# Weights made in thirds between the attention's steps, and four raw weight loads moved behind the chunks' loads

## The chip, the cores and the metric

The kernel runs on one core of a Trainium2 chip. The metric is the device time of one execution in microseconds (us). A core has TensorE (PE, the matrix engine), VectorE (DVE), ScalarE (ACT), GpSimd (POOL) and SyncE (SP, whose queue issues the loads here). Each engine works through its own instructions in the order in which the program gives them, and waits on semaphores for what other engines or DMAs produce.

## The reference

Decayed linear attention over 2 x 768 tokens with 8 heads of 64, then a gated layer (512 to 1536 to 512) behind a root-mean-square norm, then a three-way maximum layer (512 to 768 to 512), all in 32-bit floats:

```python
def _attn_ref(q, k, v, lam) -> np.ndarray:
    ...
    for b in range(nb):
        sl = slice(b * block, (b + 1) * block)
        qb, kb, vb = (q[:, :, sl], k[:, :, sl], v[:, :, sl])
        intra = np.einsum('bhic,bhjc->bhij', qb, kb) * Dmask[None]
        intra = np.einsum('bhij,bhjd->bhid', intra, vb)
        inter = np.einsum('bhid,bhde->bhie', qb * lam_pow[None], kv_state)
        out[:, :, sl] = intra + inter
        rev_pow = lam[:, None, None] ** (block - 1 - pos[None, :, None])
        kb_dec = kb * rev_pow[None]
        kv_state = lam_block[None, :, None, None] * kv_state + np.einsum('bhsd,bhse->bhde', kb_dec, vb)
    return out.astype(np.float32)

def _moe_ref(x, w_gate, w_val, w_out, rms_g) -> np.ndarray:
    rms = np.sqrt(np.mean(x * x, axis=-1, keepdims=True) + 1e-06)
    xn = x / rms * rms_g
    g = xn @ w_gate
    silu = g * (1.0 / (1.0 + np.exp(-g)))
    val = xn @ w_val
    return (silu * val @ w_out).astype(np.float32)

def _moe2_ref(x, w1, w2, w3, w_out) -> np.ndarray:
    h = np.maximum(np.maximum(x @ w1, x @ w2), x @ w3)
    return (h @ w_out).astype(np.float32)
```

## The kernel before

**Attention.** The 1536 tokens are 12 chunks of 128. Each chunk passes nine steps: `T` turns k and q on PE (`turn`, tiles `pk`, `pq`), `C` makes scores, `a` and `b` mask them on DVE into the two halves of `A`, `M` mixes (`px`), `S` carries the state (`pS`, `S_kv`), `U` sums squares (`ms`, and `ri` on POOL), `N` norms (`pb`, `x` on DVE, `xh` on ACT) and `R` makes the rest `xl`. The steps of neighbouring chunks are interleaved in one list, and `attn_step` takes the next. All matrix products of the two layers are made of three: high part by high, high by low, low by high (`mm3`: L425, L426, L427), so every operand has a `...h` and a `...l` tile.

**First stage.** For each block of 512 tokens and each of the first six hidden tiles `f`, `hidden1` makes `pg` and `pv`, Silu (L571) and the product `sg` (L572); `split` makes `hh` on ACT and `hl` on POOL; `out1` adds into `acc`, which is drained to `acc_sb` (L454 to L456). The attention steps that the first block needs run ahead of the first stage, the others in the *gaps*: `gap()` is called twice in every product of a hidden tile and twice in `out1`. The last six hidden tiles and the maximum layer are the *second stage*: products of halves (`p`, `r`, `q`, L637), with sums of weights (`tsum`, L181, L203) and sums of x (`sums`, L494), and ACT copies `c` out of `p` and `r` (L692) that must be done before PE goes on with the same bank.

**Weights.** A weight *unit* is 128 columns or rows of a matrix, named here by matrix and tile: g1, v6, o6 are tile 1 of `w_gate`, tile 6 of `w_val`, tile 6 of `w_out`; T units are sums. It is loaded as raw integer words (`wraw`, 512 KB, three buffers, L149). `begin_unit` asks for raw loads and issues two ACT steps (L227, L228). `words_of_unit` has three parts on DVE: L188, L191 and L194, the last with POOL's add (L196). `finish_unit` copies `wh` on ACT (L157) and makes `wl` on POOL (L160), or on DVE for some sums (L173). `make_unit` does all of that for one unit after another at once (finish of the unit before, the three parts of the current one, begin of the next); `third_of_unit` does it in three calls. Before, `make_unit` is called at four attention steps and in the gaps of the first eight steps of the first stage and the next four, `third_of_unit` in all later gaps.

**Order.** There is no scheduler: the order of the code is the order on every engine. What sets it around the change is the list of attention steps at which raw words are loaded and units made (L921 to L924), the rule in `gap()` (L408 to L413), the three parts in `third_of_unit` (L250 to L252), and on the load queue the order of `loads_to` (k, q and v of a chunk: `kn`, `qn`, with three buffers each, `vn` with four, L90) and `load_to` (L149).

Of the kernel before, what the change touches and what calls it, by code (L numbers as in the profile page):

```python
# [26 lines left out]
def tile_decay_attention_swiglu_maxout(  # L27
# [85 lines left out]
    groups1 = [4, 2]  # L113
# [23 lines left out]
    stage1, stage2 = [], []  # L137
# [15 lines left out]
    def finish_unit(key, W, at):  # L153
        if key:
            wh = wpools[at].tile([P, 512], F32R, tag="wh", name="wh")
            wl = wpools[at].tile([P, 512], F32R, tag="wl", name="wl")
            nc.scalar.copy(out=wh, in_=W.bitcast(F32))  # L157
            if second_sum(key):
                return lambda: lower_of_sum(key, W, wh, wl)
            nc.gpsimd.tensor_tensor(out=wl, in0=W.bitcast(F32), in1=wh.bitcast(F32), op=ALU.subtract)  # L160
            units[key] = (wh, wl)
# [14 lines left out]
    def copy_partner():  # L176
        if stage1 and first_sum(stage1[-1][0]):
            other = partner(stage1[-1][0])
            if other not in sums_in:
                sums_in[other] = psum.tile([P, 512], I32, tag="bank", name="tsum")  # L180
                nc.scalar.copy(out=sums_in[other].bitcast(F32), in_=words[other].bitcast(F32))  # L181
# [46 lines left out]
            nc.scalar.activation(out=lo, in_=lo.bitcast(U32), func=AF.Copy, scale=2.0 ** -29)  # L228
            stage1.append((key, W, at, lo, hi))

    def make_unit():

        if stage2:
            finish_unit(*stage2.pop(0))
        if stage1:
            unit = stage1.pop(0)
            for n in range(3):
                words_of_unit(n, *unit)
            stage2.append(unit[:3])
        begin_unit()  # L240

    thirds = []

    def third_of_unit():

        if not thirds:
            done = stage2.pop(0) if stage2 else (None,) * 3
            unit = stage1.pop(0) if stage1 else (None,) * 5
            later = []
            thirds.extend([lambda: (begin_unit(), words_of_unit(0, *unit)),  # L250
                           lambda: (later.append(finish_unit(*done)), copy_partner(), words_of_unit(1, *unit)),
                           lambda: (later[0] and later[0](), words_of_unit(2, *unit), stage2.append(unit[:3]))])  # L252
        thirds.pop(0)()

# [148 lines left out]
    def gap():  # L403


        pos["gap"] += 1
        if not pos["quiet"]:
            if pos["step"] == len(steps) or pos["step"] >= groups1[0] * NBLK and pos["gap"] % 4:  # L408
                third_of_unit()
            elif pos["step"] >= groups1[0] * NBLK:  # L410
                pass
            elif (pos["gap"] + 5) % (2 if pos["step"] < groups1[0] else 4) == 0:
                make_unit()  # L413
        due.sort(key=lambda e: e[0])
        while due and due[0][0] <= pos["gap"]:
            due.pop(0)[1]()
        if gaps[0]:
            left = sum(1 for p in attn_q if p[0] <= gaps[1])
            for _ in range(-(-left // gaps[0])):
                attn_step()  # L420
            gaps[0] -= 1
# [472 lines left out]
    with tc.manual_schedule():  # L894
        nc.scalar.dma_start(out=lam8, in_=lam.rearrange("(o h) -> o h", o=1).to_broadcast([P, H]))
        loads_to(0)
        nc.scalar.dma_start(out=g_sb, in_=rms_g.rearrange("(a p) -> p a", p=P))
        make_identity(nc, ident)
        nc.vector.memset(ones, 1.0)
        nc.vector.memset(zeros, 0.0)  # L900
        nc.scalar.activation(out=mhalf, in_=zeros[:, 0:1], func=AF.Silu)
        nc.vector.memset(mhalf, -0.5)
        warm = bank("warm")
        for i in range(9):
            nc.tensor.matmul(out=warm[:, 0:P], lhsT=zeros, rhs=zeros, start=True, stop=True)
        nc.gpsimd.memset(S_kv, 0.0)
        for h in range(H):
            nc.vector.tensor_tensor_scan(
                out=Tm[:, h, :], data0=lam8[:, h:h + 1].to_broadcast([P, P]), data1=ident,
                initial=0.0, op0=ALU.mult, op1=ALU.add)  # L910
        for hf in range(2):
            nc.vector.tensor_copy(out=lamh[64 * hf:64 * hf + 64, :],
                                  in_=lam8.rearrange("p (a t) -> p t a", t=2)[64 * hf:64 * hf + 64, hf, :])
        for a in range(NP):
            nc.vector.tensor_tensor_scan(
                out=lami[:, a, :], data0=lamh[:, a:a + 1].to_broadcast([P, P]), data1=zeros,
                initial=1.0, op0=ALU.mult, op1=ALU.add)
        loads_to(1)
        for i in range(sum(1 for p in attn_q if p[0] <= CPNB + 2)):
            attn_step()  # L920
            if i in (0, 7, 8, 17, 25, 40, 41, 48):  # L921
                load_to(pos["load"] + 1)
            if i in (15, 22, 32, 47):
                make_unit()  # L924
        finish = first_stage()
        pos["step"] = len(steps)
        second_stage(finish)
# [31 lines left out]
```

## Time and profile before

| what | value |
|---|---|
| median of 3 runs | 564.85 us (564.38 to 565.11) |
| the profiled execution | 567.43 us, its span 564.5 us |
| PE busy in the span | 547.1 us (97%) |
| DVE, ACT, POOL busy | 383.1 us (68%), 272.0 us (48%), 320.7 us (57%) |
| mean granted clock of PE | 0.989 |

All rows below come from that one profiled execution; times in them count from the start of its span. A row of the timeline gives start, duration, engine, line, operation, output and inputs by the program's names, and in brackets how long the engine stood idle before it and what ended that. A row of the windows gives the busy time of each engine in one stretch, the clock granted to PE (1.00 is 2.4 GHz, 0.50 is 1.2 GHz) and the share of the DMA engines.

### The profile page before, as it was taken

To read this page: it belongs to the slowest core of one execution; us is meant where nothing else is said; L and a number is where in the kernel's file an instruction comes from. 1 tells how busy PE (TensorE), PEld (TensorE's weight loads), DVE (VectorE), ACT (ScalarE), POOL (GpSimd) and SP (SyncE) were. 2 spreads that over 40 slices of the span, in tenths; PEclk is the share of its full clock that TensorE was granted. 3 is DMA by queue.
4 is the path that set the end of the run, shared out by engine and by line. 5 is a ranking of instruction groups with operands and counts; after the bars stand their busy time and mean duration, and the time that the engine had idled before them with its cause. 6 is when DMAs were issued, how large, how long until landed. Compare 5 with 4: busy or idle time off the path is not lost.

```text
span 564.5 us, 7794 instructions
## 1 busy us (share of the span) xinstructions
PE 547.1 (97%) x2880; PEld 452.0 (80%) x2880; DVE 383.1 (68%) x583; ACT 272.0 (48%) x517; POOL 320.7 (57%) x256
## 2 busy tenths in 40 slices
PE   7979989999999999989999999999999999999997
PEld 7968767888788888778888888878888888888885
DVE  6687997423358789686676867896567567774364
ACT  3566754332354534446626455555465755552120
POOL 2577998311167677647727747687377553962050
PEclk9998999999999999989999999999999999999999
DMA  8767646000023211212312222120222322210014
GB/s 204 189 177 188 176 134 168 1 0 1 2 81 107 72 40 35 66 48 76 113 38 74 75 74 76 37 75 1 74 75 76 96 91 75 74 39 0 2 45 178
DMA packets 64646, 44.54 MB, mean 79 GB/s; under 512 B 39264, under 2 KB 60768, under 8 KB 64608
## 3 DMA queue, kind: packets, MB, share of 16 engines
q1 hardware_dynamic: 63936, 44.05, 26.6%
q8 instruction: 22, 0.36, 0.3%
q14 instruction: 16, 0.13, 0.1%
q10 hardware_dynamic: 672, 0.01, 0.1%
HBM read 40.90 MB, written 3.15 MB: 78 GB/s over the span
## 4 chain that ended last, share of the span: by engine, by line
PE 83%; DVE 9%; DMA 2%; ACT 2%; issue 1%; POOL 1%; SPq 0%; ACTq 0%; DVEq 0%
PE p L637 27%; PE r L637 7%; PE acc L425 5%; PE acc L427 5%; PE acc L426 5%; PE q L637 4%; PE acc L820 3%; PE acc L819 3%; PE acc L821 3%; PE pg L425 3%; PE pg L426 3%; PE pg L427 2%; PE pv L425 2%; PE pv L427 2%; PE pv L426 2%; PE px L322 2%
## 5 line engine op out<-in xcount | busy, mean ns | idle before, releaser
L160 POOL TENSOR_TENSOR wl<-W,wh 128x512 fp32r<-128x512 f32 x75 | 102.8, 1371 | 43.4 <-ACT wh L157 43.3
L196 POOL TENSOR_TENSOR W<-W,wraw 128x512 int32<-128x512 int32 x60 | 80.7, 1346 | 72.6 <-DVE W L194 70.8
L157 ACT CAST wh<-W 128x512 fp32r<-128x512 f32 x75 | 46.5, 620 | 68.0 <-POOL W L196 67.8
L439 POOL TENSOR_TENSOR hl<-sg,hh 128x512 fp32r<-128x512 f32 x36 | 48.8, 1356 | 43.5 <-ACT hh L438 43.5
L425 PE MATMUL acc<-hh,wh 128*128 128x512 f32 x144 | 57.2, 397 | 1.0 <-DVE xl L447 1.0
L426 PE MATMUL acc<-hl,wh 128*128 128x512 f32 x144 | 56.2, 390 | 0.0
L427 PE MATMUL acc<-hh,wl 128*128 128x512 f32 x144 | 56.1, 390 | 0.0
L637 PE MATMUL p<-xl,wh 128*128 128x512 f32 x120 | 46.7, 389 | 0.0
L637 PE MATMUL p<-xh,wh 128*128 128x512 f32 x120 | 46.7, 389 | 0.0
L637 PE MATMUL p<-xh,wl 128*128 128x512 f32 x120 | 46.7, 389 | 0.0
L227 ACT ACTIVATE W<-wraw 128x512 f32<-128x512 f32 x60 | 40.0, 667 | 9.6 <-POOL wl L160 5.6
L438 ACT CAST hh<-sg 128x512 fp32r<-128x512 f32 x36 | 22.3, 620 | 43.6 <-DVE sg L572 37.4
L228 ACT ACTIVATE wraw<-wraw 128x512 int32<-128x512 uint32 x60 | 39.7, 661 | 0.0
L439 POOL TENSOR_TENSOR hl<-m,hh 128x512 fp32r<-128x512 f32 x18 | 24.5, 1366 | 24.2 <-ACT hh L438 24.1
L637 PE MATMUL p<-yh,wh 128*128 128x512 f32 x90 | 35.0, 389 | 0.0
L637 PE MATMUL p<-yl,wh 128*128 128x512 f32 x90 | 35.0, 389 | 0.0
L637 PE MATMUL p<-yh,wl 128*128 128x512 f32 x90 | 35.0, 389 | 0.0
L692 ACT COPY c<-p 128x512 f32<-128x512 f32 x30 | 17.7, 588 | 33.5 <-PE p L637 33.4
L425 PEld LDWEIGHTS acc<-hh,wh 128*128 128x128 f32 x144 | 27.0, 188 | 7.5 <-DVE xl L447 1.8
L792 DVE TENSOR_TENSOR acc_sb<-acc,acc_sb 128x512 f32<-128x512 f32 x34 | 23.3, 690 | 14.1 <-PE acc L427 13.3
L188 DVE TENSOR_SCALAR mid<-W 128x512 f32<-128x512 f32 x37 | 25.4, 686 | 9.3 <-ACT W L227 4.7
L427 PEld LDWEIGHTS acc<-hh,wl 128*128 128x128 f32 x144 | 27.0, 188 | 5.8
(177 smaller groups left out, 1444.2 us busy)
## 6 DMA issues: line engine op xcount, KB each, us to landing
wraw<-in_moe_w_out_dram SPq DMA_DIRECT2D x18, 512.0 KB, 3.4
wraw<-in_moe_w_dram SPq DMA_DIRECT2D x18, 512.0 KB, 3.6
wraw<-in_moe_w_gate_dram SPq DMA_DIRECT2D x12, 512.0 KB, 3.6
wraw<-in_moe_w_val_dram SPq DMA_DIRECT2D x12, 512.0 KB, 3.6
kn<-in_k_dram SPq DMA_DIRECT2D x12, 256.0 KB, 4.1
qn<-in_q_dram SPq DMA_DIRECT2D x12, 256.0 KB, 4.4
vn<-in_v_dram SPq DMA_DIRECT2D x12, 256.0 KB, 4.7
out_dram<-acc_sb SPq DMA_DIRECT2D x12, 256.0 KB, 2.0
```

The source lines that it names most:

```text
L157: nc.scalar.copy(out=wh, in_=W.bitcast(F32))
L160: nc.gpsimd.tensor_tensor(out=wl, in0=W.bitcast(F32), in1=wh.bitcast(F32), op=ALU.subtract)
L188: nc.vector.tensor_scalar(out=mid[key].bitcast(F32), in0=W.bitcast(F32), scalar1=LEAST, scalar2=MOST, op0=ALU.max, op1=ALU.min)
L196: nc.gpsimd.tensor_tensor(out=W, in0=W, in1=lo, op=ALU.add)
L227: nc.scalar.activation(out=W.bitcast(F32), in_=hi.bitcast(F32), func=AF.Abs)
L228: nc.scalar.activation(out=lo, in_=lo.bitcast(U32), func=AF.Copy, scale=2.0 ** -29)
L425: nc.tensor.matmul(out=out, lhsT=wh, rhs=xh_, start=first, stop=False)
L426: nc.tensor.matmul(out=out, lhsT=wh, rhs=xl_, start=False, stop=False)
L427: nc.tensor.matmul(out=out, lhsT=wl, rhs=xh_, start=False, stop=last)
L439: nc.gpsimd.tensor_tensor(out=dst_l, in0=src, in1=dst_h.bitcast(F32), op=ALU.subtract)
L637: nc.tensor.matmul(out=ps, lhsT=w[:, ks], rhs=r[:, o + k, :], start=first and k == 0 and n == 0, stop=k == 1 and n == 2, skip_group_check= ...
L792: nc.vector.tensor_tensor(out=ps if kept else y, in0=ps, in1=y, op=ALU.add)
```

## The change

`make_unit` is gone, and every unit is made by thirds. Between attention steps there are thirteen thirds where four whole units were; in the gaps of the first steps two gaps take three thirds together, and later four gaps take three, which is the old rate. Within a unit's thirds `finish_unit` moves from the second third to the first and `begin_unit` from the first to the second, everywhere in the kernel. Raw loads are asked for at other attention steps.

```diff
--- before.py
+++ after.py
@@ -228,17 +228,6 @@
             nc.scalar.activation(out=lo, in_=lo.bitcast(U32), func=AF.Copy, scale=2.0 ** -29)
             stage1.append((key, W, at, lo, hi))
 
-    def make_unit():
-
-        if stage2:
-            finish_unit(*stage2.pop(0))
-        if stage1:
-            unit = stage1.pop(0)
-            for n in range(3):
-                words_of_unit(n, *unit)
-            stage2.append(unit[:3])
-        begin_unit()
-
     thirds = []
 
     def third_of_unit():
@@ -247,8 +236,8 @@
             done = stage2.pop(0) if stage2 else (None,) * 3
             unit = stage1.pop(0) if stage1 else (None,) * 5
             later = []
-            thirds.extend([lambda: (begin_unit(), words_of_unit(0, *unit)),
-                           lambda: (later.append(finish_unit(*done)), copy_partner(), words_of_unit(1, *unit)),
+            thirds.extend([lambda: (later.append(finish_unit(*done)), words_of_unit(0, *unit)),
+                           lambda: (begin_unit(), copy_partner(), words_of_unit(1, *unit)),
                            lambda: (later[0] and later[0](), words_of_unit(2, *unit), stage2.append(unit[:3]))])
         thirds.pop(0)()
 
@@ -409,8 +398,9 @@
                 third_of_unit()
             elif pos["step"] >= groups1[0] * NBLK:
                 pass
-            elif (pos["gap"] + 5) % (2 if pos["step"] < groups1[0] else 4) == 0:
-                make_unit()
+            else:
+                for _ in range((1, 2)[pos["gap"] % 2] if pos["step"] < groups1[0] else (0, 1, 1, 1)[pos["gap"] % 4]):
+                    third_of_unit()
         due.sort(key=lambda e: e[0])
         while due and due[0][0] <= pos["gap"]:
             due.pop(0)[1]()
@@ -918,10 +908,9 @@
         loads_to(1)
         for i in range(sum(1 for p in attn_q if p[0] <= CPNB + 2)):
             attn_step()
-            if i in (0, 7, 8, 17, 25, 40, 41, 48):
-                load_to(pos["load"] + 1)
-            if i in (15, 22, 32, 47):
-                make_unit()
+            for _ in range((15, 15, 15, 18, 20, 22, 27, 30, 34, 40, 42, 45, 47).count(i)):
+                third_of_unit()
+            load_to(pos["load"] + (0, 7, 8, 30, 39, 47, 47).count(i))
         finish = first_stage()
         pos["step"] = len(steps)
         second_stage(finish)
```

The load queue (SP), from the `vn` of chunk 4 on. `kn`, `qn`, `vn` belong to one chunk each, in order (chunks 5 and 6 and the first of 7 here); the `wraw` rows are g1 and v1. Before:

```order
L90 DMA vn_252<-in_v_dram 128x8x64
L149 DMA wraw_326<-in_moe_w_gate_dram 128x4x256
L90 DMA kn_338<-in_k_dram 128x8x64
L90 DMA qn_340<-in_q_dram 128x8x64
L90 DMA vn_342<-in_v_dram 128x8x64
L149 DMA wraw_417<-in_moe_w_val_dram 128x4x256
L90 DMA kn_430<-in_k_dram 128x8x64
L90 DMA qn_432<-in_q_dram 128x8x64
L90 DMA vn_434<-in_v_dram 128x8x64
L90 DMA kn_524<-in_k_dram 128x8x64
```

Now:

```order
L90 DMA vn_252<-in_v_dram 128x8x64
L90 DMA kn_337<-in_k_dram 128x8x64
L90 DMA qn_339<-in_q_dram 128x8x64
L90 DMA vn_341<-in_v_dram 128x8x64
L90 DMA kn_431<-in_k_dram 128x8x64
L90 DMA qn_433<-in_q_dram 128x8x64
L90 DMA vn_435<-in_v_dram 128x8x64
L149 DMA wraw_480<-in_moe_w_gate_dram 128x4x256
L90 DMA kn_522<-in_k_dram 128x8x64
```

The raw words of g1 stood ahead of chunk 5 and those of v1 ahead of chunk 6; now both chunks stand ahead of g1, and v1 comes behind chunk 7.

ACT, at the passage from the first stage to the second. `W_2152` is v6 and `W_2202` is o6; `xh<-sums` are sums of x, `sg<-pg` is the last Silu of the first stage, `c` are the copies out of `p` and `r`, `W_2103` is a sum of weights. Before:

```order
L498 CAST xh_687<-sums_2163 128x512
L498 CAST xh_687<-sums_2206 128x512
L571 ACTIVATE sg_2257<-pg_2219 128x512
L438 CAST hh_2260<-sg_2257 128x512
L157 CAST wh_2274<-W_2152 128x512
L181 COPY tsum_2278<-W_2152 128x512
L692 COPY c_2297<-p_2290 128x512
L692 COPY c_2308<-r_2301 128x512
L157 CAST wh_2310<-W_2202 128x512
L692 COPY c_2329<-p_2290 128x512
L227 ACTIVATE W_2333<-wraw_2150 128x512
```

Now (v6 is `W_2156`, o6 is `W_2207`, the sum `W_2107`; lines stand 10 or 11 lower):

```order
L488 CAST xh_692<-sums_2167 128x512
L157 CAST wh_2241<-W_2156 128x512
L181 COPY tsum_2253<-W_2156 128x512
L488 CAST xh_692<-sums_2211 128x512
L561 ACTIVATE sg_2264<-pg_2224 128x512
L428 CAST hh_2267<-sg_2264 128x512
L157 CAST wh_2289<-W_2207 128x512
L682 COPY c_2303<-p_2296 128x512
L682 COPY c_2313<-r_2306 128x512
L157 CAST wh_2323<-W_2107 128x512
L682 COPY c_2333<-p_2296 128x512
L227 ACTIVATE W_2337<-wraw_2154 128x512
```

The copy `wh` of v6 and its `tsum` now stand ahead of Silu, `wh` of o6 ahead of the first copy `c`, and `wh` of the sum between the copies.

## Rows read from the trace of the kernel before

**Rows 1.** The page's head and its first part: busy us, share, instructions.

```profile
span 564.5 us, 7794 instructions
...
PE 547.1 (97%) x2880; PEld 452.0 (80%) x2880; DVE 383.1 (68%) x583; ACT 272.0 (48%) x517; POOL 320.7 (57%) x256
```

**Rows 2.** PE's waits over the span: for what, us in total, times, longest.

```profile
PE pv L425 <- DVE x L378: 2.0, 1, 2.0
PE q L637 <- DVE acc_sb L456: 2.0, 1, 2.0
...
PE pb L376 <- POOL ri L367: 1.3, 1, 1.3
...
PE pk L273 <- DMA kn<-in_k_dram: 1.2, 1, 1.2
```

**Rows 3.** Busy times by stretch: stretch, us, busy us by engine, clock, DMA share.

```profile
41.00:48.00 7.00, 6.27 (x28) 5.38 (x29) 5.68 (x7) 3.08 (x6) 5.52 (x5) 0.54 0.80 181
...
60.00:95.00 35.00, 31.03 (x234) 24.70 (x230) 32.27 (x41) 18.79 (x41) 31.59 (x26) 1.00 0.61 160
95.00:190.00 95.00, 94.67 (x529) 77.54 (x530) 44.43 (x62) 39.04 (x77) 36.34 (x29) 1.00 0.12 39
190.00:231.00 41.00, 41.00 (x183) 33.93 (x181) 38.06 (x44) 17.38 (x33) 27.73 (x19) 1.00 0.12 39
...
241.00:246.00 5.00, 4.28 (x12) 3.39 (x13) 3.76 (x7) 2.23 (x5) 1.22 (x1) 0.66 0.00 0
```

The busy columns are PE, PE's weight loads, DVE, ACT and POOL.

**Rows 4.** Timeline of the load queue, 28 to 38 us.

```profile
28.72 0.37 SPq L149 DMA_DIRECT2D wraw<-in_moe_w_gate_dram  x1
...
37.37 0.46 SPq L90 DMA_DIRECT2D kn<-in_k_dram  x1
```

**Rows 5.** Timeline of PE at chunk 6's turn.

```profile
41.73 1.11 PE L273 MATMUL pk<-ident,kn 128*128 128x128 f32 x4 [1.16 <-DMA kn<-in_k_dram]
```

**Rows 6.** Timeline of POOL at `xl` of chunk 3.

```profile
40.84 1.27 POOL L389 TENSOR_TENSOR xl<-x,xh 128x512 fp32r<-128x512 f32 x1 [2.21 <-ACT xh L380]
```

**Rows 7.** Timeline of DVE, 33 to 71 us.

```profile
33.33 0.43 DVE L191 TENSOR_SCALAR W<-W 128x512 int32<-128x512 int32 x1
...
45.58 1.03 DVE L188 TENSOR_SCALAR W<-W 128x512 f32<-128x512 f32 x1 [1.21 <-ACT W L227]
...
68.04 1.40 DVE L191 TENSOR_SCALAR W<-W 128x512 int32<-128x512 int32 x1
...
70.09 0.69 DVE L305 TENSOR_TENSOR A<-sc,Tm 128x512 f32<-128x512 f32 x1
```

**Rows 8.** Timeline of ACT at the passage, 230 to 239 us.

```profile
230.41 0.59 ACT L571 ACTIVATE sg<-pg 128x512 f32<-128x512 f32 x1
...
233.34 0.58 ACT L692 COPY c<-p 128x512 f32<-128x512 f32 x1
...
237.65 0.62 ACT L157 CAST wh<-W 128x512 fp32r<-128x512 f32 x1 [3.25 <-POOL W L196]
```

**Rows 9.** Timeline of PE at the passage, 233 to 242 us.

```profile
233.97 0.50 PE L637 MATMUL p<-zh,wh 128*128 128x512 f32 x1
...
241.72 0.60 PE L637 MATMUL q<-xh,wh 128*128 128x512 f32 x1 [1.98 <-DVE acc_sb L456]
```

**Rows 10.** Timeline of DVE ahead of and in the passage, 204 to 241 us.

```profile
204.33 0.69 DVE L572 TENSOR_TENSOR sg<-pv,sg 128x512 f32<-128x512 f32 x1 [1.22 <-POOL zl L447]
...
227.65 1.27 DVE L456 TENSOR_TENSOR acc_sb<-acc,acc_sb 128x512 f32<-128x512 f32 x2
...
229.78 0.68 DVE L194 SCALAR_TENSOR_TENSOR W<-wraw,W 128x512 int32<-128x512 int32 x1
...
240.38 0.70 DVE L188 TENSOR_SCALAR mid<-W 128x512 f32<-128x512 f32 x1 [4.63 <-ACT sg L713]
```

**Rows 11.** The page's groups of POOL's add and `hl`: count, busy, mean ns, idle.

```profile
L196 POOL TENSOR_TENSOR W<-W,wraw 128x512 int32<-128x512 int32 x60 | 80.7, 1346 | 72.6 <-DVE W L194 70.8
L439 POOL TENSOR_TENSOR hl<-sg,hh 128x512 fp32r<-128x512 f32 x36 | 48.8, 1356 | 43.5 <-ACT hh L438 43.5
```

## The prediction

> **What bounds the kernel now.** I read the page's busy times first [rows 1]: TensorE (PE) is busy 547.1 us of the span of 564.5, so what a change of order alone can give is the 17.4 us in which PE waits, and what the clock loses beside them. Then PE's own waits [rows 2]: 1.3 us for POOL's `ri`, 1.2 us for a load of `kn`, and 2.0 us each for DVE's `x` and `acc_sb`. Third, the busy times by stretch [rows 3]: between 41 and 48 us the granted clock averages 0.54, near the lower of its two levels (1.2 of 2.4 GHz), right after the two waits for `ri` and `kn`; between 241 and 246 us it averages 0.66, after the wait for `acc_sb`. The same rows show DVE busy 32.27 of 35 us and POOL 31.59 of 35 between 60 and 95 us, with PE at 31.03: there the bound is DVE's queue. From 95 to 190 us PE is busy 94.67 of 95 us, and from 190 to 231 it never waits. So three places decide: the turn of chunk 6 at 41 us, DVE's queue to 95 us, and the passage from the first stage to the second at 231 to 246 us. PE's own instructions keep their order, and every engine executes the same set of instructions as before; only waits move.
>
> **Part 1, the loads.** The load queue is served in order. The raw words of g1 are issued at 28.72 us, when a raw buffer comes free, and chunk 5's `kn` stands right behind them; chunk 6's `kn` is issued at 37.37 behind the words of v1 [rows 4]. Its data are what PE waits 1.2 us for at 41.73 [rows 5]. After the change both chunks stand ahead of g1. Their own buffers are free by about 23 to 28 us (three buffers of `kn`, four of `vn`), so both loads go out some seven and ten us early, and this wait goes: -1.2 us. The raw words move behind three and six loads of 256 KB; g1's own buffer is free only at 28.7 us, so they lose little, and v1 is needed by PE more than ten us later. I cost the later raw words at nothing; the cover is that slot wait, and without it a raw load would come one chunk's landing later for ScalarE (ACT), 4.4 us by the time from 37.37 to the end of the wait at 41.73 [rows 4, 5], not for PE.
>
> **Part 2, thirds in the attention.** POOL's `ri` of chunk 3 stood behind the integer add and a whole unit's `wl` on POOL; PE waits 1.3 us for it [rows 2]. In thirds `wl` of g0 starts as soon as its `wh` does, some three us earlier, and the queue ahead of `ri` is shorter; chunk 5's earlier `qn` also moves the steps ahead of it by about 1 us. I take the whole 1.3 us away, and at worst 0.5. With both waits gone I take it that the clock does not fall: 6.27 busy us at a mean of 0.54 instead of 1.00 cost 6.27 x 0.46 = 2.9 us [rows 3]. Gross: 1.2 + 1.3 + 2.9 = 5.4 us. What is late next: `pg` needs `xl` of chunk 3, which POOL makes from 40.84 on [rows 6], ending at 42.11. That hangs on `pb` through `x` and `xh` and so moves by `pb`'s 1.3 to 2.2 us only, while PE would now arrive at about 40.1: a new wait between 0 and 1.7 us, taken as 1.0. PE is then some 4.4 us early at 60 us.
>
> **Part 3, DVE's queue from 45 to 95 us.** This takes part of it back. DVE runs nearly without a break there, and PE waits for it: the second half of `A` at 70.09 [rows 7], `x` for 2.0 us [rows 2]. DVE gains only what it stood still for: 1.21 us before 45.58 [rows 7], which hangs on `W`'s first ACT step behind the copy of the late `pk`, 2.7 us of standing in 60 to 95 (35 less 32.27), and what it begins earlier at 44 us. The most is therefore about 5.4 us, the least about 0.5, if the raw integer steps that now stand between the attention's steps (`L188`, `L191`, `L194` one by one) come just ahead of an `A` or `x` that PE wants. I take 3.0, nearer to the row of the 1.21 us plus the earlier start than to either end. From 95 us on PE has no wait up to 231, so 3.0 us are carried that far.
>
> A step of DVE's costs two prices: `L191` 0.43 us at 33.33 and 1.40 us at 68.04 [rows 7], the long one while POOL works. The Trainium skill ("SBUF — State Buffer", section "SBUF: two separate sides") calls the ports of these two engines an exclusive lock, held for a whole instruction, with the loser blocked. The row agrees, and this speaks against the change: three more such meetings in the stretch would cost 3 x 0.97 = 2.9 us, all that the start keeps, and the sum would be +1.6 instead of -1.3.
>
> **Part 4, inside a third.** The two ACT steps that begin a unit move from the first third to the second, and the copy `wh` from the second to the first. So `wh` stands one gap behind POOL's add instead of two: ACT now waits for POOL more often, with what is queued behind. In most places PE has well over 1 us of reserve, and I cost them at nothing (0 to 1 us for all). At 231 us there is none. Before, ACT's Silu ran at 230.41 and the copy `c` at 233.34 to 233.92, both ahead of the next `wh` at 237.65, which waited 3.25 us for POOL [rows 8]; PE started `p` 0.05 us after that copy, at 233.97 [rows 9]. After, `wh` of v6 with its `tsum` stands ahead of Silu and `wh` of o6 ahead of the copy. Call t the end of DVE's `L194` of v6, 230.46 before [rows 10]. From t it goes through POOL's add (1.35 [rows 11]), `wh`, `tsum`, `xh` and Silu (0.58 to 0.62 each by the kinds in [rows 8], less about 0.1 of overlap between neighbours) to about t + 3.6, and on through `sg` (0.69 [rows 10]), `hh` (0.62), `hl` (1.36), the add of o6 (1.35 [rows 11]), `wh` (0.62) and the copy (0.58) to about t + 8.6. `L191` now goes before four `acc_sb` steps, the last two of which ended at 227.65 + 1.27 = 228.92 [rows 10], and `L194` right behind them: with both set in, at 0.41 and 0.68 us, t is about 230.0. DVE stood twice for 1.2 us earlier in that stretch (one of the two before 204.33 [rows 10]); without either, t is 227.6. Taking t = 229.0, the copy ends at 237.6 instead of 233.9: PE loses 3.7 us there (0.05 of reserve aside). Against that, the 2.0 us at 241.72 [rows 9] go: PE arrives later than the `acc_sb` that it waited for. That `acc_sb` stood behind `mid` at 240.38, after a stop of 4.63 us [rows 10]. Net 3.7 - 2.0 = +1.7 us, with t from 227.6 to 230.0 from +0.3 to +2.7. The clock's fall after 241 us (4.28 busy us at 0.66 instead of 1.00, 1.5 us) I expect again, only earlier; it could vanish (-1.5) or be worse (+1.5).
>
> **Sum.** -3.0 + 1.7 + 0 = -1.3 us. The profiled execution took 567.43 us, 2.9 of it around the span, and lies 2.6 over the median of the runs shown (564.85); nothing in the sum hangs on that, so I put it against the median: 564.85 - 1.3, rounded to 563.5.
>
> **Rivals.** (a) *The gain stays whole.* DVE follows PE and Silu is in time: -5.0 at the start, +0.3 in the middle, 560.1 us. For it: DVE stood 2.7 us in 60 to 95. Against: PE already waited for DVE there three times. (b) *Slower: ACT is held by `wh` at 231 to 239 us.* t = 230.0 gives 2.7 us, the clock falls for longer (1.5), and DVE keeps only 1.0 of the start: +3.2, 568.0 us. It decides the sign from the point where t + 8.6 is more than the start's kept gain plus 2.0 behind 233.9, so with 1.0 kept from t = 228.3 on, with 3.0 kept from t = 230.3 on. For it: `c` had 0.05 us of reserve. (c) *DVE takes it back:* the start keeps 1.5, and the middle costs 1.7: 565.0, no change. (d) *The clock falls at 41 us as before,* since PE idles for `xl` up to 1.7 us: the start keeps 1.0 and the time is 565.5. For it: two stops of 1.3 and 1.2 were enough before; against: the 2.0 us for `x` [rows 2] left the clock of 60 to 95 at 1.00 [rows 3]. The Trainium skill ("TensorE: Matmul & The Clock Gate", section "What's actually happening") calls the low level the default, released by activity; the fall after the waits agrees, and by it (d) would need PE to be no busier there than before. (e) *It does nothing:* the added moves are hidden and c6's load was the only effect: within 0.2%, as (c).
>
> **How the numbers follow.** A measurement of this kernel can tell about 0.2%, 1.1 us, from no change; so faster is under 563.7 and slower over 566.0. Forecast 0.35 (0.25 of it faster, 0.10 the same), (a) 0.20 faster, (c) with (e) 0.22 (0.03, 0.16, 0.03), (d) 0.08 (0, 0.04, 0.04), (b) 0.15 slower. That makes faster 0.48, same 0.30, slower 0.22. The range reaches from (a) with 0.3 us more to most of (b): 559.8 to 567.3; the likeliest case's own is 562 to 565.
>
> **What would show it.** In the changed profile: no wait for `kn` on `pk` and none or little for `ri` on `pb`, the clock near 1.00 in 36 to 46 us (part 1, 2); a wait for `xl` on `pg` near 40 us under 1.7; the second half of `A` of chunk 7 at 66 to 69 instead of 70.09 (part 3); Silu at 231 to 234 and `c` ending at 236 to 239 minus the start's gain, a wait of PE for ACT's `c` or Silu near 231 to 235, and none for `acc_sb` at 241 (part 4). The forecast is wrong if PE is more than 4 us or less than 1 us early at 200 us, or if PE does not wait for ACT at the passage.

## The result and the profile after

The changed kernel takes 571.65 us (median of 6 runs, 569.01 to 572.25); the kernel before, on the same chip, 564.98 (6 runs, 564.38 to 567.22). The ratio is 1.0105 with a 95% interval of 1.0078 to 1.0131: about 6 us slower, where the forecast was 1.3 us faster, and above the top of its range (567.3). The profiled execution of the changed kernel took 572.25 us, with a span of 569.2.

In the profiles below, lines above 230 stand 10 or 11 lower than before: L415 to L417 are L425 to L427, L627 is L637, L561 is Silu (L571), L682 the copy `c` (L692), L367 is `x` (L378), L369 `xh` (L380), L378 `xl` (L389). First PE's waits in the changed kernel, as in [rows 2]:

```profile
PE p L627 <- ACT c L682: 2.7, 2, 2.2
PE pq L264 <- ACT sg L561: 2.0, 1, 2.0
PE acc L415 <- DVE xl L437: 1.5, 2, 1.0
PE px L311 <- DVE A L294: 1.4, 3, 0.6
PE pg L415 <- ACT xh L369: 1.3, 1, 1.3
PE r L627 <- ACT sg L561: 1.2, 1, 1.2
...
PE pg L416 <- POOL xl L378: 0.9, 1, 0.9
PE acc L416 <- POOL hl L429: 0.8, 1, 0.8
```

The four waits of [rows 2] are gone: `ri` and `kn` at chunk 6's turn, `x` at 79 us, `acc_sb` at 241. In their place PE waits for ACT, 5.9 us for `c` and Silu, and for `xh`, `xl` and `hl`. The busy times by stretch, as in [rows 3], and for 41 to 48 and 241 to 246 us also those of a second profile of the kernel before (the run b2_before, below), which come last, in a fence of their own:

```profile
41.00:48.00 7.00, 5.46 (x31) 4.43 (x32) 6.93 (x8) 4.47 (x9) 6.11 (x5) 0.76 0.68 174
...
60.00:95.00 35.00, 31.99 (x214) 24.76 (x212) 28.18 (x40) 18.94 (x40) 30.46 (x26) 0.95 0.58 155
...
231.00:241.00 10.00, 6.61 (x23) 4.70 (x22) 3.61 (x8) 4.69 (x10) 8.31 (x7) 0.87 0.34 107
```

```profile
41.00:48.00 7.00, 6.27 (x39) 5.19 (x40) 5.82 (x7) 3.46 (x7) 5.31 (x5) 0.76 0.75 170
...
241.00:246.00 5.00, 5.00 (x22) 4.15 (x23) 4.93 (x9) 2.37 (x5) 0.48 (x2) 1.00 0.00 0
```

In the second profile the clock averages 0.76 at 41 us where the first had 0.54, and 1.00 at 241 us where the first had 0.66. The same waits are there in both: 1.2 or 1.3 us each for `ri` and `kn`, 2.0 for `acc_sb`.

PE's instructions stand in the same order in both kernels and in all that follow (but for one or two pairs of neighbours, at 23 and 36 us), so one number tells where time is lost: the start of an instruction in one profile less its start in the second profile of before. In us, at some instructions (named by their start in that profile):

| kernel | 35 | 50 | 82 | 90 | 100 | 228 | 236 | 250 | 365 | 495 |
|---|---|---|---|---|---|---|---|---|---|---|
| before, first profile | +0.2 | +0.9 | +0.8 | +0.8 | +0.8 | +0.8 | +0.8 | +2.4 | +2.4 | +2.4 |
| changed | -0.8 | +0.0 | -0.8 | +3.1 | +1.2 | +1.2 | +6.6 | +4.7 | +5.8 | +7.1 |
| e1: load order alone | -0.5 | -2.4 | -0.4 | -0.4 | -0.4 | -0.4 | -0.4 | +1.2 | +1.2 | +1.3 |
| e3: inside of a third alone | +1.9 | +0.2 | +3.1 | +3.1 | +1.2 | +1.4 | +4.3 | +3.4 | +3.4 | +7.7 |
| e4: old inside from step 13 on | -0.8 | -0.1 | -0.9 | +1.5 | +0.4 | +0.4 | +3.9 | +2.0 | +2.0 | +3.6 |
| e5: as e4, twelve thirds | -0.7 | +0.1 | +1.2 | +1.9 | +2.4 | +2.4 | +2.6 | +2.7 | +2.7 | +2.7 |
| e13: one `wh` behind Silu | -0.8 | +0.0 | -0.9 | -0.3 | +1.4 | +1.4 | +5.3 | +3.5 | +4.6 | +6.9 |
| e14: one `wh` behind `c` | -0.6 | +0.2 | -0.7 | +3.3 | +1.4 | +1.4 | +2.7 | +2.2 | +3.3 | +5.5 |
| e16: `L188` behind `x` | -0.7 | -2.6 | -1.9 | +2.1 | +0.1 | +0.2 | +5.6 | +3.7 | +4.8 | +7.0 |
| e7: drain ahead of the third | +0.2 | -0.2 | +1.9 | +1.9 | +0.0 | +0.0 | -0.2 | -2.5 | -2.5 | -2.5 |

Up to 100 us the first profile of before, e3 and e7 execute what the second does, and yet stand 0.8, 1.2 and 0.0 us later there: that much differs between executions, and a fall of the clock at 241 us makes another 1.6 (first row). Four profiles have the changed kernel's order up to there: +1.2 (changed), +0.4 (e4), +1.4 (e14) and +2.0 (e10, below). So the change gains nothing up to 100 us, if it does not lose a little, loses 3.5 us from 228 to 250 us and 2.4 us between 350 and 495 us. In each place something now stands ahead of what PE wants. The first, at 40 us, on DVE, POOL and PE (timelines of the changed kernel):

```profile
38.83 1.42 DVE L188 TENSOR_SCALAR W<-W 128x512 f32<-128x512 f32 x1
40.28 0.69 DVE L367 TENSOR_TENSOR x<-x,pb 128x512 f32<-128x512 f32 x1
...
38.70 1.26 POOL L160 TENSOR_TENSOR wl<-W,wh 128x512 fp32r<-128x512 f32 x1 [1.82 <-ACT wh L157]
...
41.68 0.50 PE L415 MATMUL pg<-xh,wh 128*128 128x512 f32 x1 [1.32 <-ACT xh L369]
43.04 0.49 PE L416 MATMUL pg<-xl,wh 128*128 128x512 f32 x1 [0.86 <-POOL xl L378]
```

`L188` of o0 stands ahead of `x` and takes 1.42 us while POOL makes a `wl`. At 84 us and at the passage it is ACT (timelines of ACT, and the rows of PE that wait for it):

```profile
83.25 0.62 ACT L157 CAST wh<-W 128x512 fp32r<-128x512 f32 x1 [3.80 <-POOL W L196]
83.78 0.59 ACT L561 ACTIVATE sg<-pg 128x512 f32<-128x512 f32 x1
...
84.42 0.79 PE L264 MATMUL pq<-ident,qn 128*128 128x128 f32 x4 [1.96 <-ACT sg L561]
...
230.79 0.62 ACT L157 CAST wh<-W 128x512 fp32r<-128x512 f32 x1 [5.18 <-POOL W L196]
...
232.36 0.59 ACT L561 ACTIVATE sg<-pg 128x512 f32<-128x512 f32 x1
...
237.04 0.62 ACT L157 CAST wh<-W 128x512 fp32r<-128x512 f32 x1 [2.65 <-POOL W L196]
237.56 0.58 ACT L682 COPY c<-p 128x512 f32<-128x512 f32 x1
...
233.00 0.50 PE L627 MATMUL r<-ah,wh 128*128 128x512 f32 x1 [1.24 <-ACT sg L561]
238.19 0.63 PE L627 MATMUL p<-zh,wh 128*128 128x512 f32 x1 [2.15 <-ACT c L682]
```

Each time ACT stands idle at a `wh` that waits for POOL's add, with a Silu or a copy queued behind that has all it needs (PE had ended `pg` by 77.08 us, and the last `p` ahead of that copy by 236.04), and PE waits for that.

### The profile page after: what moved, and what is told of

Read it like the earlier page. It is cut to its first block, busy times and chain, and to the rows that moved or that the text cites. A ratio compares the mean times of both kernels' runs of the same rounds, so it can differ in the third digit from the quotient of the medians.

```text
span 569.2 us, 7783 instructions
## 1 busy us (share of the span) xinstructions
PE 550.1 (97%) x2880; PEld 451.9 (79%) x2880; DVE 380.3 (67%) x583; ACT 273.1 (48%) x517; POOL 320.5 (56%) x256
## 4 chain that ended last, share of the span: by engine, by line
PE 72%; POOL 9%; DVE 8%; issue 5%; ACT 3%; DMA 2%; POOLq 0%; DVEq 0%; ACTq 0%
PE p L627 24%; PE r L627 6%; PE acc L415 4%; POOL W L196 4%; PE acc L416 4%; PE acc L417 4%; PE q L627 3%; PE acc L811 3%; PE acc L809 3%; PE acc L810 3%; PE pg L415 2%; PE pv L415 2%; PE pg L416 2%; PE pg L417 2%; PE pv L417 2%
## 5 line engine op out<-in xcount | busy, mean ns | idle before, releaser
L196 POOL TENSOR_TENSOR W<-W,wraw 128x512 int32<-128x512 int32 x60 | 82.0, 1367 | 86.2 <-DVE W L194 18.4
L160 POOL TENSOR_TENSOR wl<-W,wh 128x512 fp32r<-128x512 f32 x75 | 99.7, 1329 | 42.4 <-ACT wh L157 42.2
L415 PE MATMUL acc<-hh,wh 128*128 128x512 f32 x144 | 57.8, 401 | 1.7 <-DVE xl L437 1.5
L417 PE MATMUL acc<-hh,wl 128*128 128x512 f32 x144 | 56.6, 393 | 0.0
L627 PE MATMUL p<-xh,wh 128*128 128x512 f32 x120 | 47.0, 392 | 0.5 <-ACT c L682 0.5
L627 PE MATMUL p<-xl,wh 128*128 128x512 f32 x120 | 46.9, 391 | 0.0
L627 PE MATMUL p<-xh,wl 128*128 128x512 f32 x120 | 46.8, 390 | 0.0
L188 DVE TENSOR_SCALAR mid<-W 128x512 f32<-128x512 f32 x37 | 25.4, 686 | 16.7 <-ACT W L227 9.5
L627 PE MATMUL p<-yh,wh 128*128 128x512 f32 x90 | 35.0, 389 | 0.0
L627 PE MATMUL p<-yh,wl 128*128 128x512 f32 x90 | 35.0, 389 | 0.0
L627 PE MATMUL p<-yl,wh 128*128 128x512 f32 x90 | 35.0, 389 | 0.0
L415 PEld LDWEIGHTS acc<-hh,wh 128*128 128x128 f32 x144 | 27.3, 190 | 8.6 <-DVE xl L437 2.3
L562 DVE TENSOR_TENSOR sg<-pv,sg 128x512 f32<-128x512 f32 x18 | 12.4, 689 | 30.0 <-PE pv L417 14.9
L416 PEld LDWEIGHTS acc<-hl,wh 128*128 128x128 f32 x144 | 27.4, 190 | 6.4 <-POOL hl L429 1.2
L682 ACT COPY c<-p 128x512 f32<-128x512 f32 x30 | 17.5, 584 | 30.2 <-PE p L627 30.2
```

What stands on the lines that cost most here:

```text
L188: nc.vector.tensor_scalar(out=mid[key].bitcast(F32), in0=W.bitcast(F32), scalar1=LEAST, scalar2=MOST, op0=ALU.max, op1=ALU.min)
L196: nc.gpsimd.tensor_tensor(out=W, in0=W, in1=lo, op=ALU.add)
L415: nc.tensor.matmul(out=out, lhsT=wh, rhs=xh_, start=first, stop=False)
L416: nc.tensor.matmul(out=out, lhsT=wh, rhs=xl_, start=False, stop=False)
L417: nc.tensor.matmul(out=out, lhsT=wl, rhs=xh_, start=False, stop=last)
L627: nc.tensor.matmul(out=ps, lhsT=w[:, ks], rhs=r[:, o + k, :], start=first and k == 0 and n == 0, stop=k == 1 and n == 2, skip_group_check= ...
```

## The experiments

Theory W: the loss comes from `wh` one gap behind POOL's add, ahead of what PE wants from ACT. Rival L: it comes from the load order and from units made between attention steps, which crowd DVE and POOL. Ratios are to runs of the kernel before on the same chip, with 95% intervals.

**The parts of the change.** e1 is the kernel before with the change's load order alone:

```diff
-            if i in (0, 7, 8, 17, 25, 40, 41, 48):
-                load_to(pos["load"] + 1)
+            load_to(pos["load"] + (0, 7, 8, 30, 39, 47, 47).count(i))
```

> The kernel before with the load order of the change alone (raw words of g1 behind chunk 6, v1 behind chunk 7); units are made as before. Theory W (the loss of the change comes from `wh` one gap behind POOL's add, which holds ACT's queue while it waits for POOL): the 1.2 us wait for `kn` goes, nothing new comes, so about 562 to 564.5 us, and the passage at 231 us looks as before. Rival L (the loss comes from the loads and from units made between attention steps, which crowd DVE and POOL ahead of `x` and `A`): 565 to 568 us, with new waits of PE before 95 us.

565.26 us against 565.43, ratio 0.9998 (0.9981 to 1.0015): nothing. PE's wait for `kn` is gone, the clock stays up in 41 to 48 us, and PE is 2.4 us early at 50 us; at 82 only 0.4 of it is left. Other waits stand in the place of the old one: `A` 2.8 us over the span instead of 1.8, and 0.7 for `wh` and 0.8 for `wl` (busy times, PE):

```profile
41.00:48.00 7.00, 6.55 (x57) 5.36 (x57) 6.78 (x7) 3.79 (x7) 6.27 (x6) 1.00 0.35 73
...
52.14 0.50 PE L425 MATMUL pg<-xh,wh 128*128 128x512 f32 x1 [0.71 <-ACT wh L157]
...
53.64 0.51 PE L427 MATMUL pg<-xh,wl 128*128 128x512 f32 x1 [0.76 <-POOL wl L160]
```

ACT starts that `wh` at 51.47 us, in the second profile of before at 51.88: it comes hardly earlier although PE does. The time lies at the foot of L's range and outside W's, but against the runs beside it nothing is lost, so the load order alone does not make the 6 us.

e2 puts the inside of a third back in the changed kernel, e3 puts the new inside alone into the kernel before, e4 puts it back from the thirteenth step of the first stage on:

```diff
 # e2: the changed kernel with
+            thirds.extend([lambda: (begin_unit(), words_of_unit(0, *unit)),
+                           lambda: (later.append(finish_unit(*done)), copy_partner(), words_of_unit(1, *unit)),
 # e3: the kernel before with
+            thirds.extend([lambda: (later.append(finish_unit(*done)), words_of_unit(0, *unit)),
+                           lambda: (begin_unit(), copy_partner(), words_of_unit(1, *unit)),
 # e4: e3's order where pos["step"] < 12, e2's behind it
```

> The changed kernel with the inside of a third put back (begin of a unit in the first third, `wh` in the second, so two gaps behind POOL's add); loads and thirds in the attention stay. Theory W: the waits of PE for Silu at 84 us (2.0) and at 233 (1.2), for `c` (2.7), and the small ones after 358 us (1.8 in all more than before) go: about 6 us less than the changed kernel, 563 to 566 us. Rival L: no more than 2 us less, 569 to 572 us, and PE still loses what it was ahead by before 95 us.

> The kernel before with the new inside of a third alone (`wh` in the first third, begin in the second); whole units are still made at once in the attention and the loads keep their order, so thirds start with the thirteenth step of the first stage. Theory W: the passage costs 2 us net and the waits after 358 us another 2, while the start is untouched: 567 to 570 us. Rival L: as before, 564 to 566 us.

> The changed kernel with the inside of a third put back from the thirteenth step of the first stage on; up to there everything is as in the change. Theory W: the wait of PE for Silu at 84 us stays (the start's gain is gone by 95 us), the passage and the waits after 358 us are as before: 565 to 567 us. Rival L: 569 to 572 us.

e3: 571.18 us, ratio 1.0091 (1.0061 to 1.0121). Two lines of the diff, whose effect here begins at the thirteenth step, cost by themselves nearly as much as the whole change, though in part at other places: 4.3 us of it come between 365 and 495 us, where the changed kernel loses 1.3. e4: 567.76, 1.0046 (1.0028 to 1.0064); without them late in the kernel more than half of the loss is gone. Both are on W's side, each a little above its range. e2: 569.27, 1.0064 (1.0046 to 1.0081), outside W's range and inside L's, at its foot: the old inside everywhere is 1.5 us worse than e4 by the medians, with 3.0 us of waiting for `xl` at the start. So W is not all of it. In e3 the largest single loss is late, at 496 us (ACT, PE and the clock behind it):

```profile
494.54 0.62 ACT L157 CAST wh<-W 128x512 fp32r<-128x512 f32 x1 [2.86 <-POOL W L196]
...
496.21 0.79 PE L637 MATMUL p<-xh,wh 128*128 128x512 f32 x1 [2.50 <-ACT c L692]
```

```profile
495.00:500.00 5.00, 3.79 (x10) 3.03 (x11) 1.45 (x3) 3.78 (x8) 3.76 (x3) 0.66 0.31 107
```

**Phase.** The thirteen thirds ahead of the first stage are four units and one third, so every later unit also stands one gap earlier against the products. e5 is e4 with twelve:

```diff
-            for _ in range((15, 15, 15, 18, 20, 22, 27, 30, 34, 40, 42, 45, 47).count(i)):
+            for _ in range((15, 15, 15, 18, 20, 22, 27, 30, 34, 40, 42, 45).count(i)):
```

> The changed kernel with the old inside of a third from the thirteenth step of the first stage on, and with twelve thirds instead of thirteen ahead of the first stage, so that from the thirteenth step every engine has its old order. Theory W with phase (what counts is where `wh` stands against the copies, and the thirteenth third moves all later units by one gap): the passage and all after it as before, the start as in e4: 1 to 2 us less than e4, 565 to 567 us. If only the inside of a third counts and not the phase: as e4, 567 to 568.5 us.

567.22 us, 1.0040 (1.0019 to 1.0061). The time lies where both ranges meet, for the start is 2.0 us later than in e4; the table decides. From 228 to 495 us e5 loses 0.3 us against the second profile of before: old inside and old phase. e4, old inside and new phase, loses 3.3 us there, e3, new inside and old phase, 6.3, and the changed kernel with both new 5.9. What counts is not one rule but what ends up behind a step that waits, and inside and phase both set that. e5 also leaves what the new start costs by itself with twelve thirds: 2.4 us by 100 us, and 0.40% in the ratio, clear of noise. To that extent rival L is right. e11 is e5 with the old load order:

> The kernel of e5 (thirds in the attention and the gaps of the first twelve steps, everything old behind) with the old load order. If what e5 loses by 100 us (2.4 us in the profiles) comes from the thirds on DVE and POOL: the same or 1 us more, 567 to 568.5 us, with the wait for `kn` back. If it comes from the load order: 564 to 566 us.

568.59 us, 1.0045 (1.0023 to 1.0067): the same, with the wait for `kn` back at 1.6 us. So the loss belongs to the thirds, and the load order matters little here too.

**The clock.** b2_before is the kernel before once more.

> The kernel before once more, for a second profile. If the low clock at 41 to 48 us belongs to the kernel (theory K), it is there again, with a mean granted clock of about 0.989 and about 567 us. If it comes in some executions only (rival V), the clock at 41 to 48 us is at or near 1.00 and the time is 564 to 565 us; then the 2.9 us that the prediction wanted back from it were hardly in the median.

563.84 us, clock 0.996, one execution: neither number exactly. The rows stand above. The fall at 41 us is there, but half as long, and the one at 241 us is not. Mean clocks of single executions of the kernel before lie between 0.987 (567.8 us) and 1.000 (563.6 us). So V is nearer: part of the low clock that I priced belonged to the execution. e7, which has the old order up to 200 us, has 0.76 in 41 to 48 us as well.

**Single places.** e6 keeps the new inside ahead of the first stage only. e13 and e14 put back one or two `wh` in the changed kernel, e15 both:

```diff
+            second = done[0] in (("g", 3),)            # e13; e14: ("v", 6), ("o", 6)
+            finish = lambda: later.append(finish_unit(*done))
+            thirds.extend([lambda: (second or finish(), words_of_unit(0, *unit)),
+                           lambda: (begin_unit(), second and finish(), copy_partner(), words_of_unit(1, *unit)),
```

> The changed kernel with the new inside of a third only ahead of the first stage, and the old one in all gaps; thirteen thirds as in the change. Theory W: PE's wait for Silu at 84 us (2.0, with the clock's fall behind it) goes against e4: 1 to 3 us less than e4, 565 to 567 us. Rival L: that wait comes from the crowding of DVE, and is there as in e4: 567 to 569 us.

> The changed kernel with one `wh` put back by one gap: that of g3 (tile 3 of w_gate), so that it stands behind Silu at 84 us and not ahead of it. Theory W: PE's 2.0 us for Silu go, and the clock's fall behind them (0.72 in 84 to 90 us of the changed kernel); PE is 1.5 to 3.5 us earlier at 100 us, 568.5 to 570.5 us. Rival (the loss only moves to DVE's `x`, as in e6): PE is less than 1 us earlier at 100 us, 571 to 572 us.

> The changed kernel with the `wh` of v6 and o6 put back by one gap. That of o6 then stands behind the copy `c` at the passage; that of v6 stays ahead of Silu, since the sums of x come between. Theory W: PE's 2.2 us for `c` go and the 1.2 us for Silu stay, and the clock doesn't fall there: 2 to 3 us less than the changed kernel, 568.5 to 570 us. Rival: the `acc_sb` wait of the kernel before comes back in its place (2.0 us): under 1 us less, 571 to 572 us.

> The two edits of e13 and e14 together. If the two losses are separate and add: the sum of both gains, 4 to 6 us less than the changed kernel, 566 to 568 us. If one hides the other: no better than the better of the two.

e6: 567.89 us, 1.0052 (1.0033 to 1.0070), no better than e4: the time is in L's range, but the wait for Silu at 84 us, which L keeps, is gone, and other waits have taken its place. e13: 570.82, 1.0101 (1.0065 to 1.0137), no better than the change. At 90 us PE is 3.4 us earlier than in the changed kernel, at 100 us 0.2 us later, as the rival has it. In between PE waits for `x` of the next chunk, which ends at 93.90 us, and then the clock falls (DVE, PE, busy times):

```profile
86.53 0.69 DVE L274 TENSOR_TENSOR qs<-pq,lami 128x512 f32<-128x512 f32 x1 [2.25 <-ACT qT L270]
...
93.21 0.69 DVE L369 TENSOR_TENSOR x<-x,pb 128x512 f32<-128x512 f32 x1
...
93.95 1.86 PE L289 MATMUL sc<-qT,kT 64*128 64x128 f32 x14 [1.24 <-DVE x L369]
...
94.00:98.00 4.00, 4.00 (x20) 3.35 (x21) 0.00 (x0) 1.04 (x2) 2.17 (x2) 0.57 0.46 142
```

In the changed kernel the clock falls earlier, right behind the wait for Silu, and PE comes to that place at 95.30 us and does not wait for `x`:

```profile
84.00:88.00 4.00, 3.58 (x13) 3.00 (x14) 1.90 (x4) 3.10 (x6) 3.40 (x3) 0.60 0.44 131
```

The second profile of before has the same wait of 1.24 us for that `x`, from 93.36 to 94.05, and no fall of the clock behind it. So the wait for Silu is what W says, but taking it away gains nothing by 100 us: `x`, ahead of which DVE stood 2.25 us for ACT's copy `qT`, is late next, and in this execution the fall of the clock only moved there. e14: 569.57, 1.0076 (1.0052 to 1.0099). The 2.2 us for `c` at the passage are gone, and the wait for `acc_sb` of the kernel before is back with 1.4 us:

```profile
243.09 0.50 PE L629 MATMUL q<-xh,wh 128*128 128x512 f32 x1 [1.43 <-DVE acc_sb L448]
```

By 250 us PE is 2.5 us earlier than in the changed kernel, of which 1.5 are left at 495: at 376 us it waits 1.4 us for `xl`, where the changed kernel waits 0.5. e15: 569.67, 1.0066 (1.0041 to 1.0091), as e14: they don't add.

e8 and e16 test the new waits at 40 to 43 us. e8 moves one third by an attention step (41 in place of 40), e16 only its `L188`:

> The changed kernel with one third moved by one attention step (41 instead of 40), so that DVE's `L188` of o0 comes behind `x` of chunk 3 and not ahead of it. Theory S (that one step, 1.42 us long while POOL makes a `wl`, is what PE waits for at 40 to 43 us through `x`, `xh` and `xl`): the waits of `pg` for `xh` (1.3) and `xl` (0.9) shrink to under 1 us together and PE is 1 to 1.5 us earlier at 50 us; whether that reaches the end depends on Silu at 84 us: 570 to 571.5 us. Rival: `xl` was late for another reason (POOL's own queue), and PE is no earlier at 50 us; 571 to 572 us.

> The changed kernel with DVE's `L188` of o0 issued one attention step later, behind `x` of chunk 3, and nothing else moved (in e8 the `wh` of v0 moved along and put a `wl` ahead of `xl` on POOL). Theory S: `x` is 1.3 us earlier, the waits of `pg` for `xh` and `xl` (2.2 together) shrink to about 1, and the clock may not fall at 44 us: PE 1 to 3 us earlier at 50 us. How much of it is left behind Silu at 84 us is open: 569 to 571.5 us. Rival: `xl` is late on POOL all the same, and PE gains under 0.5 us at 50 us.

e8: 572.86, 1.0128 (1.0099 to 1.0157), a miss: `x` came 1.3 us earlier, but `wh` of v0 moved too, and its `wl` now stands ahead of `xl` on POOL, for which PE waits 3.0 us. e16 moves nothing else: 570.02, 1.0094 (1.0064 to 1.0124). `L188` comes behind `x`, PE waits 1.06 us for `xl` alone, and the clock does not fall (DVE, PE, busy times):

```profile
39.04 0.69 DVE L368 TENSOR_TENSOR x<-x,pb 128x512 f32<-128x512 f32 x1
39.65 0.70 DVE L188 TENSOR_SCALAR W<-W 128x512 f32<-128x512 f32 x1
...
42.00 0.50 PE L417 MATMUL pg<-xl,wh 128*128 128x512 f32 x1 [1.06 <-POOL xl L379]
```

```profile
41.00:48.00 7.00, 6.00 (x53) 5.12 (x53) 6.93 (x8) 4.75 (x11) 6.37 (x6) 1.00 0.76 200
```

PE is 2.6 us ahead at 50 us, as the forecast had it, and 0.1 us behind at 100.

**A better order.** In the kernel before, PE's 2.0 us at 241 us come from a drain that stands behind `mid` on DVE. e7 issues the drain of a later group ahead of the gap's third, e9 adds the change's load order, e10 does e7's edit in the changed kernel:

```diff
-            if m % 2:
+            if m == 1 or m == 3 and not (f == f1 and f0):
                 gap()
...
                         drain1(acc, g, j)
+                        if g:
+                            gap()
```

> The kernel before with one edit: where a group of the first stage after the first drains `acc` into `acc_sb`, the drain is issued ahead of the gap's third instead of behind it. At the passage DVE then doesn't hold the drain behind `mid`, whose operand ACT makes late. If PE's 2.0 us at 241 us and the clock's fall behind them are paid by every execution: 2 to 3.5 us less than before, 562 to 563.5 us. If something else is late next (ACT's Silu of the second stage): under 1 us less.

> The kernel before with the drain of `acc` ahead of the gap's third (as in e7) and the change's load order: the two parts that cost nothing. If they add: e7's gain of 2.5 to 3 us, and 0 to 1 us from the loads, 561 to 562 us. If the loads' new waits for `A` and `wh` weigh more: 562 to 563 us.

> The changed kernel with the drain of `acc` ahead of the gap's third. Theory W: at the passage PE waits for ACT's Silu and copies, not for `acc_sb`, so the edit that gives the kernel before 2.6 us gives under 1 us here: 570.5 to 572 us. Rival: the drain is late here too, behind the waits for ACT, and the edit gives about 2 us: 569 to 570 us.

e7: 561.79 us, 0.9946 (0.9929 to 0.9963); e9: 561.83, 0.9931 (0.9902 to 0.9961). Both beat both kernels. In e7 the drains come first and PE goes on without a stop (DVE, then PE):

```profile
236.74 2.73 DVE L456 TENSOR_TENSOR acc_sb<-acc,acc_sb 128x512 f32<-128x512 f32 x4 [3.99 <-PE acc L427]
239.39 0.68 DVE L188 TENSOR_SCALAR mid<-W 128x512 f32<-128x512 f32 x1
...
238.58 0.39 PE L639 MATMUL q<-xh,wh 128*128 128x512 f32 x1
```

e10: 568.44, 1.0046 (1.0029 to 1.0064), some 3 us less than the change by the ratios, below both ranges and nearer to the rival's. The reason is the chain itself. The edit also moves the drain before that one, ahead of `L194` of v6, in front of a `sums` step, and that step then took 0.68 us (at 226.39) where it had taken 1.67 (at 224.33 in the changed kernel). `L194` ends at 227.67 instead of 229.00, and ACT starts the copy `c` 1.3 us earlier by that, at 236.24 instead of 237.56. Silu is in time again, and PE waits 1.5 us for `c` instead of 1.2 for Silu and 2.2 for `c`; the clock stays at 1.00 from 231 to 246 us, where the changed kernel has 0.87 and then 0.92. The rows of `L194` in the changed kernel and in e10:

```profile
228.32 0.68 DVE L194 SCALAR_TENSOR_TENSOR W<-wraw,W 128x512 int32<-128x512 int32 x1
```

```profile
226.99 0.68 DVE L194 SCALAR_TENSOR_TENSOR W<-wraw,W 128x512 int32<-128x512 int32 x1
```

## Why the prediction was wrong, point by point

The sum was -3.0 us for the start, +1.7 for the passage and 0 for all other places. Against the second profile of before the three measure +1.2, +3.5 and +2.4 us (7.1 in all), against the first +0.4, +1.9 and +2.4 (4.7). The step that failed most is the gain that the start was to keep (parts 2 and 3); the next is the places that were put at nothing.

**Part 1, the loads: right on the wait, wrong on its worth.** The wait for `kn` went. e1 shows that this is worth 2.4 us at 50 us, with the clock up, and nothing at the end, since waits for `wh` and `wl` at 52 to 54 us take nearly all of it back.

**Part 2, the waits and the clock: mis-sized.** The waits for `ri` and `kn` went as forecast. The 2.9 us for the clock were read from one execution. The sentence that nothing hangs on its being 2.6 us over the median was a mistake: that execution had a longer fall at 41 us and another at 241 us. With 0.76 the same sum is 6.27 x 0.24 = 1.5 us, and the changed kernel, also at 0.76, got none of it. The new wait ahead of `xl`, taken as 1.0 and at most 1.7, measured 1.32 + 0.86 = 2.2 us, because `L188` of o0 came ahead of `x` and took 1.42 us. Part 3 had named that as a danger for the stretch after 45 us; I had not looked for it at 40 us, where it was. e16 shows that step: with `L188` behind `x` the start's gain at 50 us is there. `L188` took 1.42 us in the changed kernel beside a `wl`, and 0.42 in e8, where POOL stood idle until 40.95 (DVE, POOL of e8):

```profile
39.61 0.42 DVE L188 TENSOR_SCALAR W<-W 128x512 f32<-128x512 f32 x1
...
40.95 1.28 POOL L160 TENSOR_TENSOR wl<-W,wh 128x512 fp32r<-128x512 f32 x1 [3.99 <-ACT wh L157]
```

The Trainium skill ("SBUF — State Buffer", section "SBUF: two separate sides") calls the pair of ports that DVE and POOL share an exclusive lock; these two times agree.

**Part 3, DVE's queue: the step that failed.** The forecast kept 3.0 us of 4.4 to 100 us and beyond; measured is none, rather a loss (+1.2, within the spread). Where a lead is made it does not last: 2.4 us at 50 us in e1 are 0.4 at 82, and 2.6 in e16 are 1.9 at 82 and -0.1 at 100. Rival (c) had the reason in part. In the second profile of before and in e13 PE comes to the `x` of the stretch's end 1.24 us too soon, and that `x` ends at 94.05 and 93.90 us; so by e13, without a stop at 84 us, PE could have kept the difference of the two, 0.15 us. In the changed kernel it is not DVE that sets the end: Silu holds PE for 1.96 us at 84 us, the clock falls, and PE comes after `x`, which ends at 94.91. An end of the range below 0.5 was left out, although thirds could put more ahead of `x`; e5, with 2.4 us lost by 100 us, is that case.

**Part 4, the passage: the mechanism right, the price against the wrong base.** t was 229.00 as taken; that it is exact is luck, for it was a choice between 227.6 and 230.0. `c` ended at 238.14 (forecast 237.6), PE lost 1.24 + 2.15 us, and the wait for `acc_sb` went. e14, with one `wh` behind the copy, and e10, with `L194` 1.3 us earlier, each take part of this away. Against the first profile of before the net is 2.28 - 0.41 = 1.9 us (the starts of the same instruction at 250 and 228 us; forecast 1.7). Against the second it is 3.5, since there the clock did not fall at 241 us and there was nothing to win back.

**The other places: put at nothing, measured 2.4 us.** "In most places PE has well over 1 us of reserve, and I cost them at nothing (0 to 1 us for all)" came out at 2.0 us of waiting at 84 us, which is part of why the start kept nothing, and at 2.4 us lost between 350 and 495 us. By the starts that is 1.1 us at 361.83, behind a wait of 0.79 for `hl`, 0.5 at 378.01, behind 0.47 for `xl`, and 0.8 at 491.65, behind 0.54 for `c` (POOL, ACT, PE of the changed kernel):

```profile
359.25 1.30 POOL L196 TENSOR_TENSOR W<-W,wraw 128x512 int32<-128x512 int32 x1 [4.50 <-DVE W L194]
...
489.97 0.62 ACT L157 CAST wh<-W 128x512 fp32r<-128x512 f32 x1 [2.94 <-POOL W L196]
...
361.83 0.50 PE L416 MATMUL acc<-hl,wh 128*128 128x512 f32 x1 [0.79 <-POOL hl L429]
...
491.65 0.50 PE L627 MATMUL p<-xh,wh 128*128 128x512 f32 x1 [0.54 <-ACT c L682]
```

The copy `c` stands behind a waiting `wh` again. `hl` stands on POOL right behind the add at 359.25, for which POOL waits for DVE: the same stop one engine on. I had read reserves of single instructions, and not what a queue of work behind one waiting step does to them. e3 shows how far that can go: 2.50 us and the clock's fall in one place.

**Rivals.** (b) comes nearest, with its mechanism and place, at 568.0 against a measured 571.65; the late waits, and a start that kept nothing instead of 1.0, are what it lacked. Its point of decision, t = 228.3 if the start keeps 1.0, was passed (229.00). (d), the clock falling at 41 us, happened too, to 0.76.

What stays open: why e5's thirds lose 2.4 us by 100 us was not taken further apart than to the thirds, and the late losses of the changed kernel were not undone one by one; whether a waiting `wh` also makes `xl` late at 378 us is not shown.

## What to carry to other kernels

When a producer's result is copied by a shared in-order engine, count what stands behind that copy in the queue, not how long it has until its own use: moving a copy nearer to what it waits for turns slack into a stop for everything behind it. A gain ahead of a stretch that another engine bounds is worth only what that engine's own queue lets through; look for the instruction that ends the stretch, and see whether the change moves that one. A price taken from one profiled execution that lies off the median needs a second profile first.

## What the runs showed of the hardware

After the same two waits of PE at 37 to 42 us, the granted clock of 41 to 48 us was 0.54 in one execution of the kernel before and 0.76 in another; after the same 2.0 us of waiting at 241 us it was 0.66 and 1.00. That wait stands in five profiles (both of before, e1, e5, e11), and the clock fell behind it in three of them (the first of before, e1, e11). I had taken the fall as a fixed consequence of a wait.
